# Running the attention products of two half-steps in one stretch, with all eight PSUM banks in one ring

## Chip, cores, metric

One core of one Trainium2 chip. The metric is the device time of one execution in microseconds (us), the median of several. The span in a profile (first to last instruction) is some 1.8 us shorter than the time. The traces are each of one execution.

## The reference, cut to what matters

A decayed linear attention over 4 batches, 8 heads, 768 tokens in blocks of 64, followed by a dense layer with a tanh GELU:

```python
for b in range(nb):                       # blocks of 64 tokens
    intra = einsum('bhic,bhjc->bhij', qb, kb) * Dmask
    intra = einsum('bhij,bhjd->bhid', intra, vb)
    inter = einsum('bhid,bhde->bhie', qb * lam_pow, kv_state)
    out[:, :, sl] = intra + inter
    kv_state = lam_block * kv_state + einsum('bhsd,bhse->bhde', kb_dec, vb)
x = out.transpose(0, 2, 1, 3).reshape(3072, 512)
return gelu(x @ w_in) @ w_out             # 512 -> 2048 -> 512
```

## The kernel before

The kernel works in 24 steps. A step is half of the heads of one superblock of 256 tokens. Each step has an attention stretch on TensorE: `scores` (S), the key-value products (K), the products of the masked scores of the step before with v (O), and the products with the carried state. S, K and O use 64x64 tiles of the array; the state products use all 128x128. PSUM is the memory that TensorE writes its products to; the kernel deals it out in eight banks, each with room for 128x512 fp32 numbers, and a bank can be written anew only when its last reader is done.

```python
ps_S = tile_pool(name="psS", bufs=1, space=PSUM)     # scores: two banks of their own
ps_M = tile_pool(name="psM", bufs=6, space=PSUM)     # everything else: six banks

def R(n, s):                  # one stretch: scores of n, products of n and s = n - 1
    scores(n)
    products(n, s)            # K of n, O and state products of s; then x_out on ScalarE
    causal(n)                 # VectorE masks the scores: one instruction of 128x1024
    ...
    update(n, 0)              # VectorE takes K into the state, GpSimd spreads it

for n in range(8, NSTEP + 1):
    ...
    prep(n + 2)               # q, k, v of step n+2 to fp16; q and k transposed by a DMA
    fill(2 if n <= 12 else 4) # so many pieces of the dense layer
    R(m, n - 1)
    fill(1)
    U(m)
    fill(2 if n in (8, 11) or n > 12 and n % 2 else 3)
```

Between the stretches `fill` issues pieces of the dense layer for the tokens that are done. A piece is about 0.87 us of TensorE. A group of two superblocks has 30 of them: 16 pieces of the first matmul (bank Hps, emptied by the GELU on ScalarE into gT) and then, twice, seven products named by their banks A, A, B, B, C, D, D. The second matmul is done in a Strassen-like form, with seven products in place of eight, so VectorE must first form sums of blocks of gT:

```python
G_SUMS = {5: ..., 2: ..., 1: ..., 7: ..., 6: ...}     # five sums; B needs 5 and 2, C needs 1, D 7 and 6
behind(9, 0, 4)       # behind piece 9: the five sums of blocks 0..3  (128x1024 each)
behind(13, 4, 6)      # behind piece 13: the five sums of blocks 4, 5 (128x512)
behind(n1, 6, 8)      # behind piece 16: the five sums of blocks 6, 7 (128x512)
```

## Time and profile before

| | before |
|---|---|
| median time | 205.1 us (204.85 to 205.55, 3 runs) |
| span of the profiled run | 202.8 us |
| busy: TensorE / VectorE / ScalarE / GpSimd | 96% / 72% / 53% / 33% |
| TensorE waits listed from 75 to 200 us | none |

A busy share of 96% alone is not proof, because matmuls overlap and their ends are modelled. In this study I use "pause" for the distance from one matmul's start to the next one's, less the time that the first needs to stream (216, 109 or 56 ns for 512, 256 or 128 columns). The waits that the profile lists are a little shorter, as they count from the modelled end.

This is VectorE's timeline over the two stretches of a group whose sums are being formed (start, length, instruction, count):

```profile
120.10 1.23 DVE L299 TENSOR_TENSOR PT<-Sps,mask 128x1024 f16<-128x1024 f32 x1 [4.72 <-PE Sps L290]
121.24 0.46 DVE L387 SCALAR_TENSOR_TENSOR t<-t,lamu,OK 128x64 f32<-128x64 f32 x2
122.25 4.01 DVE L469 TENSOR_TENSOR gs<-gT 128x1024 f16<-128x1024 f16 x5 [0.55 <-ACT gT L426]
126.18 0.68 DVE L240 TENSOR_TENSOR qk<-q,dq 128x512 f16<-128x512 f32 x1
126.79 1.75 DVE L469 TENSOR_TENSOR gs<-gT 128x512 f16<-128x512 f16 x5
128.46 1.21 DVE L299 TENSOR_TENSOR PT<-Sps,mask 128x1024 f16<-128x1024 f32 x1
...
130.40 2.72 DVE L469 TENSOR_TENSOR gs<-gT 128x512 f16<-128x512 f16 x4
```

### The profile page before, as it was taken

The numbers are of one execution on the slowest core, as the hardware profiler recorded it, in microseconds if no ns is written. First come the engines' busy times: TensorE is split into PE (matmuls) and PEld (weight loads), VectorE is DVE, ScalarE is ACT, GpSimd is POOL, SyncE is SP. The second block draws the span as 40 slices with busy tenths as digits, with TensorE's granted clock in tenths as the row PEclk, the third lists the DMA queues.
The fourth block names the chain that finished last, engine by engine and source line by source line (L and its number), as shares of the span: only waits on it lengthen the run. The fifth ranks groups of instructions, "written<-read, shape, count | busy, mean of one in ns | idle before, by whom it ended". The sixth has DMA issues, their size and how long they took to land.

```text
span 202.8 us, 5650 instructions
## 1 busy us (share of the span) xinstructions
PE 194.7 (96%) x2348; PEld 129.2 (64%) x2348; DVE 146.1 (72%) x281; ACT 108.1 (53%) x205; POOL 66.7 (33%) x80
## 2 busy tenths in 40 slices
PE   6888999999999999999999999999999999999993
PEld 1456544456887888654688654788554788545882
DVE  5896623889999989939997738996739673136653
ACT  2475778375793473487632477641576431666210
POOL 6593132457475354136135404315412100000000
PEclk9999999999999999999999999999999999999999
DMA  6999999999999999698669974775230003300014
GB/s 175 291 330 387 383 387 376 291 289 318 289 254 224 294 238 293 129 276 191 67 167 201 301 187 123 89 173 148 83 88 0 3 0 107 105 0 0 3 45 162
DMA packets 64201, 37.85 MB, mean 187 GB/s; under 512 B 17584, under 2 KB 59568, under 8 KB 64176
## 3 DMA queue, kind: packets, MB, share of 16 engines
q1 hardware_dynamic: 63344, 36.97, 71.3%
q10 hardware_dynamic: 832, 0.52, 0.9%
q8 instruction: 18, 0.29, 0.6%
q14 instruction: 7, 0.06, 0.1%
HBM read 27.26 MB, written 6.29 MB: 165 GB/s over the span
## 4 chain that ended last, share of the span: by engine, by line
PE 80%; DMA 10%; SPq 4%; ACT 2%; issue 1%; DVE 1%; ACTq 0%
PE Hps L422 34%; PE MD L493 8%; PE MB L493 8%; PE MA L493 7%; PE O2ps L437 6%; PE MC L493 4%; SPq L69 4%; DMA wi<-in_moe_w_in_dram 4%; DMA qkT<-qk 3%; PE Hps L539 3%; DMA out_dram<-o 3%; PE Sps L290 3%; PE OK L348 3%; PE OK L339 2%; ACT gT L426 1%
## 5 line engine op out<-in xcount | busy, mean ns | idle before, releaser
L422 PE MATMUL Hps<-xT,w_in 128*128 128x512 f16 (+1 forms) x416 | 79.1, 346 | 0.0
L426 ACT ACTIVATE gT<-Hps 128x512 f16<-128x512 f32 x88 | 52.2, 600 | 24.2 <-PE Hps L422 23.4
L422 PEld LDWEIGHTS <-w_in 128*128 128x128 f16 x416 | 40.1, 98 | 33.4
L394 POOL TENSOR_TENSOR u<-t,lumask 128x256 f16<-128x256 f32 x40 | 29.2, 734 | 81.9 <-DVE t L387 58.9
L469 DVE TENSOR_TENSOR gs<-gT 128x512 f16<-128x512 f16 (+1 forms) x74 | 43.3, 645 | 11.8 <-ACT gT L426 11.6
L493 PEld LDWEIGHTS <-gs 128*128 128x128 f16 x400 | 38.6, 98 | 4.7 <-DVE gs L469 0.3
L299 DVE TENSOR_TENSOR PT<-Sps,mask 128x1024 f16<-128x1024 f32 x24 | 29.2, 1216 | 13.1 <-PE Sps L290 13.1
L230 POOL TENSOR_TENSOR v<-v,dv 128x512 f16<-128x512 f32 x24 | 29.2, 1218 | 5.0 <-DMA v<-in_v_dram 3.3
L367 ACT ACTIVATE xT<-OK 128x256 f16<-128x256 f32 x47 | 18.2, 459 | 18.0 <-PE OK L348 14.6
L500 ACT ACTIVATE m<-MB 128x512 f32<-128x512 f32 x10 | 6.0, 597 | 27.7 <-PE MB L493 27.7
L493 PE MATMUL MA<-w_sum,gT 128*128 128x256 f16 x160 | 19.5, 273 | 0.1
L245 ACT ACTIVATE qk<-k 128x512 f16<-128x512 f32 x24 | 15.1, 629 | 8.1 <-DMA k<-in_k_dram 8.1
L493 PE MATMUL MD<-w_sum,gs 128*128 128x256 f16 x152 | 19.4, 273 | 0.0
L493 PE MATMUL MB<-w_out,gs 128*128 128x256 f16 x160 | 19.3, 273 | 0.0
L493 PEld LDWEIGHTS <-gT 128*128 128x128 f16 x160 | 15.5, 98 | 3.2 <-ACT gT L426 0.5
L240 DVE TENSOR_TENSOR qk<-q,dq 128x512 f16<-128x512 f32 x23 | 17.3, 754 | 0.0
L504 DVE TENSOR_TENSOR o<-MA,m 128x512 f32<-128x512 f32 x10 | 6.9, 686 | 12.0 <-ACT m L500 12.0
L387 DVE SCALAR_TENSOR_TENSOR t<-t,lamu,OK 128x64 f32<-128x64 f32 x64 | 14.7, 272 | 0.6
L437 PE MATMUL O2ps<-w_out,gT 128*128 128x512 f16 x64 | 14.6, 379 | 0.0
L128 DVE TENSOR_TENSOR w_sum<-w_out 128x1024 f16<-128x1024 f16 x10 | 8.9, 926 | 6.5 <-POOL w_out L118 3.5
L290 PEld LDWEIGHTS <-qkT 64*64 64x64 f16 x384 | 6.1, 106 | 8.8 <-issue 4.2
L290 PE MATMUL Sps<-qkT 64*64 64x128 f16 x384 | 10.0, 222 | 1.1 <-DVE qkT L266 0.5
(59 smaller groups left out, 158.1 us busy)
## 6 DMA issues: line engine op xcount, KB each, us to landing
q<-in_q_dram SPq DMA_DIRECT2D x24, 256.0 KB, 4.8
k<-in_k_dram SPq DMA_DIRECT2D x24, 256.0 KB, 4.8
v<-in_v_dram SPq DMA_DIRECT2D x23, 256.0 KB, 5.3
out_dram<-o SPq DMA_DIRECT2D x22, 256.0 KB, 3.4
wo<-in_moe_w_out_dram SPq DMA_DIRECT2D x4, 1024.0 KB, 9.5
wi<-in_moe_w_in_dram SPq DMA_DIRECT2D x4, 512.0 KB, 7.6
wi<-in_moe_w_in_dram SPq DMA_DIRECT2D x2, 1024.0 KB, 12.5
v<-in_v_dram ACTq DMA_DIRECT2D x1, 256.0 KB, 4.3
```

The source lines that it names most:

```text
L230: pin(nc.gpsimd.tensor_tensor(wide(tv[:]), ld32[s][2][:], decay(dv, s), ALU.mult))
L240: pin(q_eng.tensor_tensor(wide(tq), q32[:], decay(dq, s), ALU.mult))
L245: pin(nc.scalar.activation(out=wide(tk), in_=k32[:], func=AF.Copy))
L290: pin(nc.tensor.matmul(Sps[half64(c), hl, hp, jk, :], o[half64(hl), 1, jk, hp, half64(c)], o[half64(hl), 0, :, hp, half64(c)], start=True, ...
L299: pin(nc.vector.tensor_tensor(t[:].rearrange("p a b c d -> p (a b) (c d)"), Ss.pop(n)[:].rearrange("p a b c d -> p (a b) (c d)"), mask[:]. ...
L367: pin(nc.scalar.activation(out=d, in_=o, func=AF.Copy))
L394: pin(nc.gpsimd.tensor_tensor(u[:], state[half][:].unsqueeze(2).to_broadcast([P, 2, 2, D]), lumask[:, 2 * half : 2 * half + 2, :].unsqueez ...
L422: pin(nc.tensor.matmul(by_block(Hps[:, i, :]), w_in16[:, c, f * P : (f + 1) * P], x(c), start=(c == 0), stop=(c == NC - 1)))
L426: pin(nc.scalar.activation(out=dst, in_=Hps[:], func=AF.Gelu_apprx_tanh))
L437: pin(nc.tensor.matmul(O2[tau][0][:], gT[:, f % HF, f // HF, tau * P : (tau + 1) * P], w_out16[:, f, :], start=(n == 0), stop=(n == NF - 1)))
L469: pin(nc.vector.tensor_tensor(gsum[m][:, i, :], block(T0, F0, i), block(T1, F1, i), op))
L493: pin(nc.tensor.matmul(dst, lhsT, rhs, start=(i == 0), stop=(i == HF - 1), skip_group_check=True))
```

## The change

From step 10 on the two steps of a superblock go through one stretch, a burst: S of both, O of the two steps before, K of both, state products. This halves the number of changes between 64x64 and 128x128 tiles. A burst needs four banks for scores, two for O and two for K, so the two pools become one of eight banks, the score tile becomes two tiles, and the masking of a step becomes two instructions. The pieces between are dealt out anew.

```diff
-    ps_S = ctx.enter_context(tc.tile_pool(name="psS", bufs=1, space=PSUM))
-    ps_M = ctx.enter_context(tc.tile_pool(name="psM", bufs=6, space=PSUM))
+    ps_M = ctx.enter_context(tc.tile_pool(name="psM", bufs=8, space=PSUM))
 ...
+    def burst(ns, ss):
+        for n in ns:
+            scores(n)
+        O = [ps_M.tile([P, 2, 2, P], FP32, tag="M", name=f"O{c}") for c in range(2)]
+        ... # O of both ss
+        if ns:
+            K = [ps_M.tile([P, 2, P], FP32, tag="M", name=f"K{c}") for c in range(2)]
+        ... # K of both ns, then the state products of both ss
+        for n in ns:
+            causal(n)
+        for i, s in enumerate(ss):
+            x_out(s, [t[:, i].rearrange("p h t -> p (h t)") for t in O])
+        ...
+        for n in ns:
+            update(n, 0)
 ...
-    for n in range(8, NSTEP + 1):
-        ...
+    ... # steps 8 and 9 singly
+    for n in range(10, NSTEP + 1, 2):
+        ns = (n, n + 1) if n < NSTEP else ()
+        if n + 2 < NSTEP:
+            prep(n + 2)
+        fill(0 if n == 12 else 2)
+        burst(ns, (9,) if n == 10 else (n - 2, n - 1))
+        fill(2)
+        for m in ns:
+            U(m)
+        fill(2)
+        if n + 3 < NSTEP:
+            prep(n + 3)
+        fill(5 if n == 10 else 13 if n % 4 else 5)
```

More of the change, by code (lines that the diff above doesn't have):

```diff
@@ L285, in scores @@
         o = qkT[n]
-        Sps = ps_S.tile([P, 2, 2, 2, P], FP32, tag="S", name="Sps")
+        Sps = [ps_M.tile([P, 2, 2, P], FP32, tag="M", name=f"S{hl}") for hl in range(2)]
         for hp in range(2):
@@ L290, in scores @@
                     pin(nc.tensor.matmul(
-                        Sps[half64(c), hl, hp, jk, :], o[half64(hl), 1, jk, hp, half64(c)],
+                        Sps[hl][half64(c), hp, jk, :], o[half64(hl), 1, jk, hp, half64(c)],
                         o[half64(hl), 0, :, hp, half64(c)], start=True, stop=True,
@@ L298, in causal @@
         t = ptp.tile([P, 2, 2, 2, P], FP16, tag="PT", name=f"PT_{n}")
-        pin(nc.vector.tensor_tensor(
-            t[:].rearrange("p a b c d -> p (a b) (c d)"),
-            Ss.pop(n)[:].rearrange("p a b c d -> p (a b) (c d)"),
-            mask[:].unsqueeze(1).to_broadcast([P, 4, 2 * P]), ALU.mult))
+        for hl, Sps in enumerate(Ss.pop(n)):
+            pin(nc.vector.tensor_tensor(
+                t[:, hl].rearrange("p b c d -> p b (c d)"), Sps[:].rearrange("p b c d -> p b (c d)"),
+                mask[:].unsqueeze(1).to_broadcast([P, 2, 2 * P]), ALU.mult))
         PTs[n] = t
@@ L328, in products @@
                             start=start(c, hl), stop=(jk == 1), skip_group_check=True))
-            Kps[n] = OK
+            Kps[n] = [t[:, 256:384] for t in OK]
         if s is None:
@@ L353, in products, with start @@
         return OK, opened
+    def burst(ns, ss):
+        for n in ns:
+            scores(n)
+        O = [ps_M.tile([P, 2, 2, P], FP32, tag="M", name=f"O{c}") for c in range(2)]
+        seen = set()
+        def start(kind, c, hl):
+            new = (kind, c, hl) not in seen
+            seen.add((kind, c, hl))
+            return new
+        qTs = [qkT.pop(s) for s in ss]
+        for i, s in enumerate(ss):
+            PT, tv = PTs.pop(s), a16.pop(s)[2]
+            for hp in range(2):
+                for jk in range(2):
+                    for c, hl in TILES:
+                        pin(nc.tensor.matmul(
+                            O[c][half64(hl), i, hp, :], tv[half64(c), jk, 2 * hp + hl, :],
+                            PT[half64(c), hl, hp, jk, :], start=start("O", c, hl), stop=False,
+                            skip_group_check=True))
+        if ns:
+            K = [ps_M.tile([P, 2, P], FP32, tag="M", name=f"K{c}") for c in range(2)]
+        for i, n in enumerate(ns):
+            _, tk, tv = a16[n]
+            last = (n // 2) % NSB == NSB - 1
+            for jk in range(2):
+                for hp in range(2):
+                    for c, hl in TILES:
+                        if c == 1 and last:
+                            continue
+                        pin(nc.tensor.matmul(
+                            K[c][half64(hl), i, hp * D : hp * D + D],
+                            tk[half64(c), jk, 2 * hp + hl, :], tv[half64(c), jk, 2 * hp + hl, :],
+                            start=start("K", c, hl), stop=(jk == 1), skip_group_check=True))
+            Kps[n] = [t[:, i] for t in K]
+        for i, s in enumerate(ss):
+            for c in range(2):
+                if c == 0 and (s // 2) % NSB == 0:
+                    continue
+                u = us.pop((s, 0) if c else (s - 2, 1))
+                for hp in range(2):
+                    pin(nc.tensor.matmul(O[c][:, i, hp, :], u[:, hp].rearrange("p l d -> p (l d)"),
+                                         qTs[i][:, 0, :, hp, half64(c)], start=False, stop=True,
+                                         skip_group_check=True))
+        for n in ns:
+            causal(n)
+        for i, s in enumerate(ss):
+            x_out(s, [t[:, i].rearrange("p h t -> p (h t)") for t in O])
+        sbg = ss[-1] // 2
+        g, i = group_of[sbg]
+        if i == len(groups[g]) - 1:
+            queue_group(g)
+        for n in ns:
+            update(n, 0)
@@ L379, in update @@
         if "t" in parts:
-            OK = Kps[s] if c == 0 else Kps.pop(s)
-            K = OK[c][:, 256:384].rearrange("p (hp d) -> p hp d", hp=2)
+            K = (Kps[s] if c == 0 else Kps.pop(s))[c].rearrange("p (hp d) -> p hp d", hp=2)
             t = ucp.tile([P, 2, D], FP32, tag=f"t{half}", name=f"t_{s}_{c}")
@@ L711 @@
     fill(2)
-    for n in range(8, NSTEP + 1):
-        m = n if n < NSTEP else None
-        if m is not None:
-            stage_t(n)
+    stage_t(8)
+    prep(10)
+    fill(2)
+    R(8, 7)
+    fill(1)
+    U(8)
+    fill(2)
+    prep(11)
+    fill(2)
+    R(9, 8)
+    fill(1)
+    U(9)
+    fill(3)
+    for n in range(10, NSTEP + 1, 2):
+        ns = (n, n + 1) if n < NSTEP else ()
         if n + 2 < NSTEP:
             prep(n + 2)
-        fill(2 if n <= 12 else 4)
-        R(m, n - 1)
-        fill(1)
-        if m is not None:
-            U(m)
-        fill(2 if n in (8, 11) or n > 12 and n % 2 else 3)
+        fill(0 if n == 12 else 2)
+        burst(ns, (9,) if n == 10 else (n - 2, n - 1))
+        fill(2)
+        for m in ns:
+            U(m)
+        fill(2)
+        if n + 3 < NSTEP:
+            prep(n + 3)
+        fill(5 if n == 10 else 13 if n % 4 else 5)
     fill(len(filler))
```

## The prediction

> **What bounds the kernel now.** I read the page's busy shares and clock first, then the chain of waits, then TensorE's waits in the part that the change touches, and last the timeline around one attention stretch.
>
> ```profile
> PE 194.7 (96%) x2348; PEld 129.2 (64%) x2348; DVE 146.1 (72%) x281; ACT 108.1 (53%) x205; POOL 66.7 (33%) x80
> PEclk9999999999999999999999999999999999999999
> PE 80%; DMA 10%; SPq 4%; ACT 2%; issue 1%; DVE 1%; ACTq 0%
> ```
>
> TensorE is busy for 96% of the span, at full clock, and is 80% of the chain. A busy TensorE says little by itself, as its ends are modelled; the chain says more:
>
> ```profile
> 82.86 0.87 PE MD L493 x8
> 83.73 6.04 PE Hps L422 x28
> 89.78 0.35 PE Sps L290 x16
> 90.12 0.12 PE OK L325 x16
> 90.25 0.23 PE OK L339 x16
> 90.47 0.22 PE OK L348 x2
> 90.69 6.04 PE Hps L422 x28
> 96.73 0.35 PE Sps L290 x16
> ```
>
> From 77 us to the end every piece of the chain is a matmul, and each begins where the one before ended. Asked for TensorE's waits from 75 to 200 us, the profile lists none. So in the stretch where the change acts (step 10 starts at about 70 us) the time is the sum of TensorE's start-to-start times, and two things alone can change it: fewer nanoseconds between matmuls, or a wait that was not there. The 216 ns from one 128x512 matmul to the next (6.04 / 28) is streaming; it can't shrink. What is not streaming stands at the two ends of an attention stretch (64x64 tiles between 128x128 ones). Two narrow windows of TensorE's timeline show the starts:
>
> ```profile
> 89.40 0.38 PE L422 MATMUL Hps<-xT,w_in 128*128 128x512 f16 x1
> ```
>
> ```profile
> 90.25 0.22 PE L339 MATMUL OK<-PT,v 64*64 64x128 f16 x3
> 90.41 0.28 PE L348 MATMUL OK<-qkT,u 128*128 128x128 f16 x2
> 90.53 0.38 PE L422 MATMUL Hps<-xT,w_in 128*128 128x512 f16 x1
> ```
>
> With the first score matmul at 89.71, the entry takes 309 ns in place of 216: 93 ns lost. The second group of four scores comes 80 ns after the first, where the later ones are 56 ns apart: 24 more. The exit, from the last group of four (90.25) to the first 128x128 matmul (90.41), takes 158 ns where 56 would do: 102 lost. The matmul after that comes 66 ns on: 10 more. One stretch thus pays 93 + 24 + 102 + 10 = 229 ns for going into small tiles and back.
>
> **What the Trainium skill says.** "TensorEngine Tiling (Array Packing)", section Key Properties, says that changing the tiling mode drains the TensorE, while tiles within one mode run independently. The trace agrees: 93 and 102 ns at the two changes, and almost nothing between the scores, the K products and the O products, all in 64x64 tiles. "TensorE: Matmul & The Clock Gate", section Back-to-back issue gap, gives N / 2.4 + 2.5 ns; 216 and 56 ns for 512 and 128 columns agree. "PSUM — Partial Sum Buffer", section The four PSUM rules, has 8 banks and at most one per matmul output; no trace shows the count, but it is what the change spends whole. "SBUF — State Buffer", section Who interferes with whom, says that a VectorE instruction with two SBUF inputs contends with a GpSimd instruction that reads SBUF. The trace agrees: five sums of 128x512 took 1.75 us from 126.79 on with GpSimd quiet, and five took 3.06 us from 130.40 on with GpSimd at work.
>
> **The change part by part.**
> Removed: from step 8 on the kernel before has 17 stretches (16 steps and one closing). Afterwards there are 2 single ones (8, 9) and 8 bursts (10, 12, ... 24), so 7 fewer: 7 x 0.229 = 1.6 us of TensorE time, all of it on the path. The matmuls themselves stay, and so do the pieces of the dense layers between. The start up to step 7 keeps its order; only the score tile becomes two tiles in the common pool.
> Added on VectorE: the masking of one step becomes two instructions. Consecutive 128x512 fp32 ones start 0.60 us apart (133.98, 134.58, 135.18), while the one of 128x1024 takes 1.14 us (128.46 to 129.60). So 0.06 us per step, 1.4 us over 24 steps, on an engine at 72%: nothing on the path by itself.
> Moved: a burst with both halves takes 4 score banks, 2 for O and 2 for K, all eight. Before, the scores had two banks of their own, so six others always came from the ring. Now each bank of a burst must be given up by its last reader first, and the first pieces after it need its score banks, which VectorE has to mask. From the built kernel I took who wrote each bank last and who reads it last. A burst that starts at T has its scores done at T+0.47 (8 groups x 56 ns + 24), its O products at T+0.92, K then takes 0.26 (8 x 32 ns), and exit and state products 0.55.
>
> The tight places are bursts 12, 16 and 20, which stand directly behind the products A and B of a dense group. There one bank is the one of A, and its last reader is the second of VectorE's two output sums, which needs ScalarE's copies of B:
>
> ```profile
> 132.74 0.27 PE L493 MATMUL MB<-w_out,gs 128*128 128x256 f16 x1
> ```
>
> ```profile
> 133.05 0.60 ACT L500 ACTIVATE m<-MB 128x512 f32<-128x512 f32 x1 [2.38 <-PE MB L493]
> 133.54 0.38 ACT L501 ACTIVATE m<-MB 128x256 f32<-128x256 f32 x1
> ```
>
> ScalarE starts 0.31 us after the last B matmul starts, which is T+0.11. Its first copy ends at T+0.71, VectorE's first sum runs from T+0.75, the second from T+1.35 to T+2.02. Bank A is free at about T+2.05.
> Burst 20: K's second bank is A's. It is wanted at T+0.92 and free at T+2.05: 1.13 us of standstill. Afterwards the score banks are masked in time.
> Burst 12: the same 1.13 us; then VectorE also has the q of step 14 (0.6 us) ahead of its masking, so the first score bank comes free at T+3.25, while TensorE wants it at T+2.86: 0.4 more, 1.5 in all.
> Burst 16: K's second half isn't computed there, and bank A goes to the piece behind the burst, wanted at about T+1.83: 0.2, with 0.1 for bank B: 0.3.
> Bursts 10, 14, 18, 22 and 24 stand behind dense pieces whose banks ScalarE has long emptied: none.
> Sum of these: 1.5 + 0.3 + 1.1 = 2.9, rounded to 3.0.
>
> Also moved: a burst needs the transposed q and k of two steps at its start. From issue to landing the transposes take 3.1 / 4.5 / 6.9 us (least, median, most). Step 11's landed at 70.43 in the trace before, and the burst wants it at 70.2. Step 13's is issued only after four dense pieces behind burst 10, and burst 12 starts about 9.5 us after burst 10: a margin from +1 to -2 us. And behind bursts 14 and 18 VectorE has four maskings, updates and ten sums in a row, so the last sums may come after the product that needs them. I put these together at 0.5 us, since most have some slack and waits at burst 12 overlap.
>
> Total: 205.1 - 1.6 + 3.0 + 0.5 = 207.0; I record 206.8, a little nearer to no loss, because the piece counts with their special cases (0 at step 12, 5 at step 10, 13) look tuned on the chip.
>
> **Rivals.** First: the waits are absorbed and the saving stands alone, 205.1 - 1.6 = 203.5. For it: VectorE is idle for 28% of the span, and no TensorE wait shows now. Against it: the last A sum is bound by latency and not by load, and nothing before the burst can hurry it. Second: VectorE becomes the local bound, for from 80 to 110 us it is busy 25.94 of 30 us. Then the pieces behind every burst wait for masking or sums, 0.5 to 1 us more at five bursts, and the time is 209 to 211. Against it: from 140 to 170 us it is busy 19.50 of 30. Third: late transposes hold bursts 12 and 14 by 1 to 3 us each: 208 to 210. For it: the 6 us landings around 76 and 88 us; against: fewer loads are in flight then.
>
> **Range and chances.** The floor is 203.5, where all waits vanish; I can find no second saving, so faster by over 2% (under 201.0) gets 0.02. Over 2% slower (above 209.2) needs 5.7 us of waits, nearly twice the firm ones: 0.10. Within 2%: 0.88. The range is 203.7 to 209.2.
>
> **What would show it.** Ten stretches from step 8 on, each with about 93 and 102 ns at its ends; a TensorE wait of about 1.1 us at the K products of bursts 12 and 20, put down to VectorE's output sum; masking instructions of about 0.67 us; and the waits adding up to about 3 us. No wait above 0.3 us at a burst would make the first rival right; waits on transposes at steps 11, 13 or 15 the third; waits of dense pieces for masking or sums at most bursts the second. A cost per stretch other than 229 ns would show the saving mis-sized.

## The result and the profile after

| | before | after |
|---|---|---|
| median time | 204.97 us (204.24 to 205.55, 4 runs) | 212.12 us (211.53 to 213.02, 4 runs) |
| ratio | | 1.0354 (95%: 1.0303 to 1.0406) |
| span of the profiled run | 202.8 us | 211.2 us |
| stretches from step 8 on | 17 | 10 |

Ratios are the mean time of one kernel's runs over that of the other's runs of the same rounds, so they are not quite the ratios of the medians. Executions over 1.5% slower than the fastest of the same kernel are left out of the means. The change made the kernel 7.1 us slower.

The page of the kernel after, busy shares and the chain:

```profile
PE 196.7 (93%) x2348; PEld 130.8 (62%) x2348; DVE 152.0 (72%) x305; ACT 107.2 (51%) x205; POOL 66.8 (32%) x80
PE 63%; DVE 23%; DMA 6%; SPq 4%; issue 3%; ACT 1%; DVEq 0%
```

TensorE was 80% of the chain and is now 63%; VectorE was 1% and is 23%. So in parts of the run VectorE sets the pace. TensorE's waits over the whole run, longest in total first (us in total, times, longest):

```profile
PE MB L549 <- DVE gs L525: 3.9, 2, 2.2
PE S L289 <- DMA qkT<-qk: 2.1, 2, 1.6
PE idle L154 <- DVE ones L148: 1.5, 1, 1.5
PE K L387 <- DVE o L561: 0.8, 1, 0.8
```

The third belongs to the start and was there before, and of the second the kernel before had one wait of 0.4 us, at about 63 us. The others are new. The new pauses from step 10 on, from the starts in TensorE's timeline, in the first profile and in a second profile of the same kernel (run after_again); those under 0.2 us are left out:

| pause of TensorE | what it waits for | first profile | second |
|---|---|---|---|
| product B behind burst 14 | VectorE's block sum gs | 2.35 | 1.78 |
| product B behind burst 18 | the same | 1.86 | 1.98 |
| burst 10, scores of step 11 | DMA transpose of q and k | 0.69 | 0.64 |
| burst 12, scores of step 13 | the same | 1.74 | 2.59 |
| burst 14, scores of step 15 | the same | none | 0.68 |
| burst 20, K | bank of A, VectorE's output sum | 1.03 | 1.03 |
| behind burst 16 | the same | 0.22 | 0.22 |
| sum | | 7.9 | 8.9 |

Less the 7 x 0.229 = 1.6 us saved, the second profile should be 7.3 us over the span before; it is 210.5 - 202.8 = 7.7. In the first, 6.3 is expected and 8.4 found, and 1.7 of the rest is a fall of the clock: from 107.7 to 111.0 us the granted clock was half.

```profile
107.70:111.00 3.30, 3.30 (x18) 2.30 (x16) 1.89 (x3) 1.34 (x3) 0.00 (x0) 0.50 0.07 19
```

(Window; busy time and count of TensorE, its weight loads, VectorE, ScalarE, GpSimd; then the clock, here 0.50, and the DMA share.) Sixteen matmuls started 0.104 us too late there, 1.7 us in all. It isn't the cause of the slowdown: the second profile has a clock of 1.000, and its time, 212.26 us, is no shorter than the kernel's median.

The longest pause, in TensorE's timeline and then in VectorE's. Burst 14 starts at 93.03:

```profile
103.34 0.82 PE L549 MATMUL MB<-w_out,gs 128*128 128x256 f16 x6
106.35 1.26 PE L549 MATMUL MB<-w_out,gs 128*128 128x256 f16 x10 [2.19 <-DVE gs L525]
```

```profile
93.49 2.48 DVE L299 TENSOR_TENSOR PT<-S,mask 128x512 f16<-128x512 f32 x4 [3.87 <-PE S L289]
95.89 0.84 DVE L443 SCALAR_TENSOR_TENSOR t<-t,lamu,K 128x64 f32<-128x64 f32 x4
96.66 3.83 DVE L525 TENSOR_TENSOR gs<-gT 128x1024 f16<-128x1024 f16 x5
100.41 0.84 DVE L443 SCALAR_TENSOR_TENSOR t<-t,lamu,K 128x64 f32<-128x64 f32 x4
101.17 1.00 DVE L239 TENSOR_TENSOR qk<-q,dq 128x512 f16<-128x512 f32 x1
102.09 5.20 DVE L525 TENSOR_TENSOR gs<-gT 128x512 f16<-128x512 f16 x9
```

VectorE stands idle for 3.87 us before the burst, because the next instruction in its order, a masking, waits for the scores (experiment 5 shows that other work was ready), and then works without a break for over 13 us. Six matmuls of B are done by 103.34 + 6 x 0.109 = 103.99; the seventh needs the sum of block 6, which is the sixth of the row that starts at 102.09. The chain of waits gives those six 4.13 us, 0.69 each in the mean. In the kernel before, five such sums took 1.75 us (126.79), 0.35 each. GpSimd's timeline of the same stretch of the kernel after shows what runs beside them, and VectorE's, in narrow windows, shows that the mean hides two kinds of sums:

```profile
101.01 1.63 POOL L450 TENSOR_TENSOR u<-t,lumask 128x256 f16<-128x256 f32 x2 [2.88 <-DVE t L443]
...
102.61 1.22 POOL L229 TENSOR_TENSOR v<-v,dv 128x512 f16<-128x512 f32 x1
```

```profile
102.85 1.26 DVE L525 TENSOR_TENSOR gs<-gT 128x512 f16<-128x512 f16 x1
...
105.21 0.41 DVE L525 TENSOR_TENSOR gs<-gT 128x512 f16<-128x512 f16 x1
```

The first three of the six stand beside a GpSimd instruction each and end 0.28 to 0.29 us after it (102.92, 104.11 and 105.29, after 102.64, 103.82 and 105.00). From the start of each to the next one's are 0.76, 1.18 and 1.18 us; from 105.21 on, with GpSimd quiet, 0.34.

The other two pauses that matter, burst 12 (second half of the scores) and burst 20 (K):

```profile
79.91 0.42 PE L289 MATMUL S<-qkT 64*64 64x128 f16 x16
81.90 0.42 PE L289 MATMUL S<-qkT 64*64 64x128 f16 x16 [1.57 <-DMA qkT<-qk]
```

```profile
148.44 0.21 PE L387 MATMUL K<-v,qk 64*64 64x64 f16 x1
149.48 0.44 PE L387 MATMUL K<-v,qk 64*64 64x64 f16 x31 [0.83 <-DVE o L561]
```

### The profile page after: what moved, and what is told of

Read it like the earlier page. It is cut to its first block, busy times and chain, and to the rows that moved or that the text cites. A ratio compares the mean times of both kernels' runs of the same rounds, so it can differ in the third digit from the quotient of the medians.

```text
span 211.2 us, 5685 instructions
## 1 busy us (share of the span) xinstructions
PE 196.7 (93%) x2348; PEld 130.8 (62%) x2348; DVE 152.0 (72%) x305; ACT 107.2 (51%) x205; POOL 66.8 (32%) x80
## 4 chain that ended last, share of the span: by engine, by line
PE 63%; DVE 23%; DMA 6%; SPq 4%; issue 3%; ACT 1%; DVEq 0%
PE Hps L478 23%; DVE gs L525 9%; PE MD L549 8%; PE O2ps L493 7%; PE MB L549 6%; PE MA L549 5%; DVE PT L299 4%; PE MC L549 4%; SPq L68 4%; DMA wi<-in_moe_w_in_dram 3%; PE Hps L595 3%; DVE qk L239 3%; DVE t L443 2%; DMA qkT<-qk 2%; PE S L289 1%
## 5 line engine op out<-in xcount | busy, mean ns | idle before, releaser
L450 POOL TENSOR_TENSOR u<-t,lumask 128x256 f16<-128x256 f32 x40 | 28.4, 725 | 78.8 <-DVE t L443 46.3
L525 DVE TENSOR_TENSOR gs<-gT 128x512 f16<-128x512 f16 (+1 forms) x74 | 44.1, 658 | 9.2 <-ACT gT L482 9.2
L549 PEld LDWEIGHTS <-gs 128*128 128x128 f16 x400 | 39.4, 100 | 10.5 <-DVE gs L525 5.0
L299 DVE TENSOR_TENSOR PT<-S,mask 128x512 f16<-128x512 f32 x48 | 30.1, 680 | 12.3 <-PE S L289 12.3
L229 POOL TENSOR_TENSOR v<-v,dv 128x512 f16<-128x512 f32 x24 | 29.8, 1253 | 5.0 <-PE OK L324 1.7
L239 DVE TENSOR_TENSOR qk<-q,dq 128x512 f16<-128x512 f32 x23 | 20.5, 900 | 0.0
L424 ACT ACTIVATE xT<-O 128x256 f16<-128x256 f32 x30 | 10.7, 459 | 9.1 <-PE O L398 8.1
L289 PE MATMUL S<-qkT 64*64 64x128 f16 x384 | 9.4, 221 | 2.8 <-DMA qkT<-qk 2.1
L549 PE MATMUL MC<-w_sum,gs 128*128 128x256 f16 x80 | 11.0, 283 | 0.1
```

Source lines behind the costliest of these rows:

```text
L229: pin(nc.gpsimd.tensor_tensor(wide(tv[:]), ld32[s][2][:], decay(dv, s), ALU.mult))
L239: pin(q_eng.tensor_tensor(wide(tq), q32[:], decay(dq, s), ALU.mult))
L289: pin(nc.tensor.matmul(Sps[hl][half64(c), hp, jk, :], o[half64(hl), 1, jk, hp, half64(c)], o[half64(hl), 0, :, hp, half64(c)], start=True, ...
L299: pin(nc.vector.tensor_tensor(t[:, hl].rearrange("p b c d -> p b (c d)"), Sps[:].rearrange("p b c d -> p b (c d)"), mask[:].unsqueeze(1).t ...
L424: pin(nc.scalar.activation(out=d, in_=o, func=AF.Copy))
L450: pin(nc.gpsimd.tensor_tensor(u[:], state[half][:].unsqueeze(2).to_broadcast([P, 2, 2, D]), lumask[:, 2 * half : 2 * half + 2, :].unsqueez ...
```

## The experiments

Three theories after the result. **A**: the main loss is VectorE coming late with the block sums behind bursts 14 and 18, because the burst moves two maskings and two updates ahead of them, and perhaps because GpSimd then reads at the same time. **B**: the loss is in the banks: a burst wants all eight, or the common ring or the split masking costs by itself. **C**: transposes come late, because a burst wants two at once. All kernels below gave correct results unless it is said.

### Experiment 1: the urgent sums first

To the kernel after:

```diff
             behind(9, 0, 4)
-            behind(13, 4, 6)
-            behind(n1, 6, 8)
+            behind(13, 4, 6, (5, 2))
+            behind(n1, 6, 8, (5, 2))
+            behind(n1 + 1, 4, 8, (1, 7, 6))
```

> The changed kernel with the last sums of a dense group in another order: the two that the next two products need come first, the three others after them, in three instructions in place of six. Theory A (the main loss is VectorE reaching these sums too late, in its unbroken row of work behind bursts 14 and 18; 2.35 and 1.86 us in the trace): both waits of MB for gs fall to under 0.3 us and the time falls by about 4 us, to 208. Theory B (the loss is in the eight banks that a burst needs): nothing to win here, 212. Theory C (transposes that come late): 212 too.

Measured: 210.74 us (209.58 to 211.53), 1.0256 of before (1.0198 to 1.0315). B's pauses fell to 1.48 and 1.03, not to 0.3. The wanted sum is now the third of its row, not the sixth, but those three took 3.19 us (104.05 to 107.24): the first ended 0.28 us after GpSimd's spreading of the state, the other two 0.28 us after a scaling of v each. Theory A in part, and a hint that the neighbour and not only the order counts.

### Experiment 2: transposes earlier

To the kernel after, `prep(n + 3)` directly behind the burst, and `prep(11)` directly behind step 8:

```diff
         burst(ns, (9,) if n == 10 else (n - 2, n - 1))
+        if n + 3 < NSTEP:
+            prep(n + 3)
         fill(2)
         for m in ns:
             U(m)
         fill(2)
-        if n + 3 < NSTEP:
-            prep(n + 3)
```

> The changed kernel with the casts and the transpose of step n+3 placed directly behind burst n in place of four dense pieces later, and those of step 11 two pieces earlier. Theory C (bursts 10 and 12 wait for the transposed q and k of their second half, 0.69 and 1.74 us in the trace): both waits fall to under 0.4 us, and the time falls by up to 2.4 us, to about 210; where burst 12 no longer waits for the transpose, the wait for the bank of A that it hid may show, some 1 us, so 210 to 211. Theories A and B: no change, 212, or A a little worse because VectorE has the q ahead of the sums.

Measured: 213.56 us (212.62 to 214.34), 1.0396: no gain. TensorE's waits from 75 us on:

```profile
PE MB L549 <- DVE gs L525: 4.2, 2, 2.3
PE K L387 <- DVE o L561: 1.6, 2, 0.8
PE MC L549 <- DVE PT L299: 0.2, 1, 0.2
```

The transposes are gone from the list, but K now waits for the output sum twice: burst 12 pauses 0.97 us at K and 0.37 behind the burst, 1.34 in all. The prediction had 1.5 us for just this place. In the kernel after, that wait lay hidden behind the longer one for the transpose. The earlier `prep(11)` also made ScalarE wait for the load of k ahead of a GELU, and TensorE paused 1.85 us at 60 us; that is the edit's own fault. So theory C's waits are real, but the one at step 13 is worth far less than its length.

### Experiment 3: the ring without the bursts

The kernel before with only the pools, the score tiles and the masking of the change:

```diff
-        Sps = ps_S.tile([P, 2, 2, 2, P], FP32, tag="S", name="Sps")
+        Sps = [ps_M.tile([P, 2, 2, P], FP32, tag="M", name=f"S{hl}") for hl in range(2)]
 ... # ps_M with 8 banks, causal in two instructions, as in the change
```

> The kernel before, with only the pool part of the change: all eight banks in one ring, the scores in two tiles of it, the masking in two instructions; no bursts. If sharing the ring or the longer masking costs by itself (theory B in its wide form), the time rises by 1 us or more over 205. Theories A and C: within 0.5 us of 205.

Measured: 204.62 us (204.44 to 205.25), 0.9973 (0.9922 to 1.0024), the same as before, and no TensorE wait from 75 to 200 us. The shared ring and the split masking cost nothing. Theory B in its wide form falls.

### Experiment 4: experiments 1 and 2 together

> e1 and e2 together. If the losses are independent and A and C name them: 212 - 4.2 - 2.4 = about 205.5, with 1 to 1.3 us of bank waits (bursts 20 and 16) and the saving of 1.6 us in it. If they hide one another, 207 or more.

Measured: 210.24 us (209.39 to 210.84), 1.0233 (1.0182 to 1.0285). B's pauses are 1.48 and 1.03 as in experiment 1, K at burst 20 is 1.03, burst 12 still waits 0.97 for a transpose and then 0.37, and product B of the first group now waits 1.05 for its sums. The losses do not add; one gives way to the next.

### Experiment 5: half of the first sums before the burst

Experiment 1 with one more line changed:

```diff
-            behind(9, 0, 4)
+            behind(5, 0, 2)
+            behind(9, 2, 4)
```

> e1 with one more move: the first block of sums is cut in two, the half whose inputs are ready is done before the burst of steps 14 and 18, while VectorE stands idle there (3.9 us in the trace). Theory A (VectorE has too much to do between the burst and the product that needs the last sums): the waits of MB for gs, 2.35 and 1.86 us in the changed kernel and 1.48 and 1.03 in e1, fall below 0.3 us, and the time falls to about 208. Were the waits set by something else than VectorE's load there, they would stay at e1's 1 to 1.5 us and the time at 210.7.

Measured: 209.37 us (208.31 to 210.97), 1.022 (1.0153 to 1.0287). The waits from 86 us on:

```profile
PE K L387 <- DVE o L561: 0.8, 1, 0.8
PE MC L549 <- DVE PT L299: 0.2, 1, 0.2
```

The waits for sums are gone (one pause of 0.14 us is left at burst 14's product). Burst 12 still paused 1.1 us for its transpose. In this trace another 2.5 us were lost before 40 us, where nothing had been changed (ScalarE waited for loads of k for up to 3.1 us at a time), so it shows less than the whole gain; whether the other runs lost that too isn't on record. VectorE's idle time before the burst was the place for this work; with the load spread, the product does not wait.

### Experiment 6: bursts 16 and 20 at another place

The kernel after, with 15 and 15 pieces between bursts in place of 19 and 11:

```diff
-        fill(5 if n == 10 else 13 if n % 4 else 5)
+        fill(5 if n <= 12 else 9)
```

> The changed kernel with the dense pieces between bursts split 15 and 15 from step 14 on in place of 19 and 11, so that bursts 16 and 20 stand behind the last sum of a token block and not behind its product B. Theory B (K's bank waits for VectorE's sum of A): the waits at K of burst 20 (1.03 us) and behind burst 16 (0.22) vanish; MB's waits for gs stay near 2 us, as the place of bursts 14 and 18 is the same; so about 211. Theory A alone: 212.

Measured: 211.18 us, the median of the three fast runs (210.68 to 212.80; the fourth, 214.39, was slow), 1.0326 (1.027 to 1.0382). K's pause at burst 20 fell from 1.03 to 0.32 and the one behind burst 16 went away; B's pauses stayed at 2.48 and 2.04, and step 13's transpose at 2.25. The bank theory holds in its narrow form: the wait is set by where the burst stands behind product B, and it was worth 0.9 us at most. The median is 0.85 us below that of the kernel after (212.03, below), as forecast, but three runs that lie 2.1 us apart don't make this sure.

### Experiment 7: GpSimd without its reads

Wrong result (relative error 1.03):

```diff
-        pin(nc.gpsimd.tensor_tensor(wide(tv[:]), ld32[s][2][:], decay(dv, s), ALU.mult))
+        if s >= 10:
+            pin(nc.gpsimd.memset(tv[:], 0.0625))
+        else:
+            pin(nc.gpsimd.tensor_tensor(wide(tv[:]), ld32[s][2][:], decay(dv, s), ALU.mult))
```

> Wrong result on purpose: from step 10 on the scaling of v on GpSimd is replaced by a memset of the same tile, which reads no SBUF. If the sums come late because GpSimd's reading slows VectorE's two-input sums (ten of them took 0.65 us each in the changed kernel; 0.35 each where GpSimd was quiet before), they run at under 0.45 us, MB's waits fall from 2.35 and 1.86 to under 1 us each, and the time falls by about 3 us, to 209. If VectorE's row of work is too long whatever GpSimd does, the waits stay above 1.5 us and the time above 211.

Measured: 207.89 us (207.65 to 209.18), 1.016 (1.0121 to 1.0199), so 4.1 us less than the kernel after. The two rows of sums in the same part of VectorE's timeline:

```profile
96.55 3.83 DVE L528 TENSOR_TENSOR gs<-gT 128x1024 f16<-128x1024 f16 x5
...
102.00 3.85 DVE L528 TENSOR_TENSOR gs<-gT 128x512 f16<-128x512 f16 x10
```

The maskings, updates and the q between are within 0.02 us of the kernel after, and so are the first five sums, beside GpSimd's state spreading, which still reads. Only the last ten differ: 3.85 us, 0.385 each, where six had taken 4.13. The first of them still ended 0.28 us after the state spreading; two ran beside the memsets (102.49 to 103.47) and started the next after 0.34 us, as with GpSimd quiet. So it is the reading and not GpSimd's being at work. B's pauses fell from 2.35 and 1.86 to 0.73 and 0.20: without GpSimd's reading of v the product was late by under 1 us, with it by 2 us. What is left is not the row of VectorE in itself either. Beside the state spreading, two of the first five sums took 0.93 and 1.02 us to the next start in place of 0.60, the q 0.92 in place of 0.60 and one of the ten 0.75 in place of 0.34, 1.5 us together. That is more than the 0.73, so with no reading on GpSimd the product would not have waited: an estimate, which no run tests.

### Experiment 8: bursts from step 14 on

Steps 10 to 13 singly, as in the kernel before; sums as in experiment 5; bursts 16, 20 and 24 ahead of the second block's products:

```diff
-    for n in range(10, NSTEP + 1, 2):
+    for n in range(10, 14):
+        prep(n + 2)
+        fill(2 if n <= 12 else 4)
+        R(n, n - 1)
+        fill(1)
+        U(n)
+        fill(2 if n == 11 or n > 12 else 3)
+
+    for n in range(14, NSTEP + 1, 2):
 ...
-        fill(5 if n == 10 else 13 if n % 4 else 5)
+        fill(13 if n % 4 == 2 and n > 14 else 5)
```

> A version meant to keep the saving and lose the waits: bursts only from step 14 on (so no transpose is wanted early), bursts of steps 16, 20 and 24 placed ahead of the second token block's products, the sums ordered as in e5. 12 stretches from step 8 on in place of 17 save 5 x 0.229 = 1.1 us. If theories A, B and C name all the waits: 203.9, against 205 before. Any wait left is added to that: with 1 us of rest it equals the kernel before.

Measured: 206.58 us (206.38 to 208.53), 1.0105 (1.0053 to 1.0156). No transpose wait after step 9, but the group around burst 14 still waits for sums, 0.49, 0.30 and 0.78 us, and small pauses add up to some 1 us. Most of the loss is gone, not all of it.

### The kernel after once more

> The changed kernel once more, unaltered, for a second profile: in the first one TensorE's clock fell for 3.4 us behind the longest wait. If the waits are the kernel's own, the same four places wait again for about the same times (sums 2.4 and 1.9 us, transposes 0.7 and 1.7, the bank of A 1.0), whatever the clock does, and the time is 211.5 to 212.5.

Measured: 212.03 us (211.46 to 212.26), 1.034 (1.0307 to 1.0373). The same places wait; the figures are in the table above, and the transpose of step 15 comes to them. The clock was 1.000 throughout.

### Experiment 9: bursts from step 16 on

As experiment 8, with steps 10 to 15 singly, each five or six pieces apart.

> e8 with bursts only from step 16 on, where e8 still waited for sums of the group of step 14: 13 stretches in place of 17, a saving of 4 x 0.229 = 0.9 us. If no wait is left beyond those of the kernel before, 204.0 to 204.4 against 205; if the sums and banks still cost what they cost in e8, 205.5 to 206.

Measured: 205.85 us (204.91 to 206.6, 6 runs), 1.0044 (1.0011 to 1.0077): a little slower than the kernel before. New pauses of 0.60 (A waits for the output sum of D), 0.32 and 0.24 us take back the 0.9 us saved, and this trace also lost 1 us more than that of before at the start. The hoped-for gain did not come.

### Experiment 10: the opposite of the change

The kernel before, from step 10 on with a dense piece between scores and products:

```diff
         if n is not None:
             scores(n)
+        if n is not None and n >= 10:
+            fill(1)
         products(n, s)
 ...
-        fill(2 if n <= 12 else 4)
+        fill((2 if n <= 12 else 4) - (10 <= n < NSTEP))
```

> The kernel before with the opposite of the change: from step 10 on one dense piece is taken from ahead of the scores and put between the scores and the products, so that each of 14 steps goes into small tiles twice. If a stretch costs 0.2 to 0.23 us of TensorE time and nothing else matters, the time rises by 14 x 0.2 to 0.23 = 2.8 to 3.2 us, to about 208, and TensorE shows no new waits. If the cost per stretch is only an appearance of modelled ends, the time stays at 205.

Measured: 208.17 us (207.25 to 208.72), 1.0156 (1.0118 to 1.0195), 3.3 us more, and no TensorE wait from 75 us on. The pauses of TensorE from step 10 on add up to 6.78 us where they were 3.84 (a group of four 64x64 matmuls counted as one, pauses over 8 ns): 2.94 for 14 more stretches, 0.21 each. One of the split steps:

```profile
128.65 0.42 PE L290 MATMUL Sps<-qkT 64*64 64x128 f16 x16
129.00 1.04 PE L422 MATMUL Hps<-xT,w_in 128*128 128x512 f16 x4
129.96 0.32 PE L325 MATMUL OK<-v,qk 64*64 64x64 f16 x16
130.11 0.40 PE L339 MATMUL OK<-PT,v 64*64 64x128 f16 x16
```

Sixteen scores take 0.35 us to the next piece, and four matmuls of 512 columns take 0.96 where 4 x 0.216 = 0.86 would do: the two changes of tile size, a tenth of a microsecond each. The cost per stretch is real time.

### Experiment 11: a control

The kernel before with the sums of experiment 5.

> The kernel before with only the reordered sums of e5, without ring and bursts: a control for e8 and e9. It has no wait for sums, so nothing to win: within 0.5 us of 205, or a little worse.

Measured: 204.71 us (204.27 to 205.99, 6 runs), 0.9999 (0.9965 to 1.0033): the same. The order of the sums is worth nothing where nothing waits for them, so what it won in experiments 1 and 5 is repair of a loss that the bursts made.

No version beat the kernel before.

## Why the prediction was wrong

**The bound: right.** TensorE's start-to-start times set the time before. Experiment 11 and experiment 3 fit: other work on VectorE or in the banks, as long as nothing waits, changes nothing. ("To the end" is a little too wide: the chain is of matmuls up to 199.4 us, and the last 3.4 us are an output sum and its store.)

**The saving, 7 x 0.229 = 1.6 us: right.** The kernel after has 10 stretches from step 8 on, with 0.09 us lost at a clean entry and about 0.1 at every exit. Experiment 10 adds 14 stretches and pays 0.21 us of pauses each. By this count there was never more than this to win.

**The split masking off the path: right.** Four took 2.40 us to the next instruction, 0.60 each as worked out, and experiment 3 shows it costing nothing. In the row behind a burst it adds 4 x 0.60 - 2 x 1.14 = 0.12 us.

**The bank waits, 3.0 us: right in mechanism, too large in sum.** Burst 20: 1.13 predicted, 1.03 measured. Burst 16: 0.3 predicted, 0.22 measured. Burst 12: 1.5 predicted, nothing seen, because a longer wait for the transpose stood ahead of it and the bank was free by then; experiment 2 took that wait away and 1.34 us of the predicted one appeared. So 1.25 in place of 3.0.

**The step that failed is "I put these together at 0.5 us", for late transposes and late sums.** They measured 2.4 + 4.2 = 6.6 us in the first profile and 3.9 + 3.8 = 7.7 in the second. The text had named both and waved both through with "most have some slack". Nothing was added up for the sums, though the trace before had every duration: 4 maskings x 0.60, 8 updates x 0.20, five sums 4.01, the q 0.61, and six sums at 0.61 to 0.35 give 2.4 + 1.6 + 4.0 + 0.6 + 2.1 to 3.7 = 10.7 to 12.3 us. From the first masking at T + 0.46 that is T + 11.2 to 12.8, against a product that wants its sum at T + 10.96 (103.99 - 93.03, in the trace after): 0.2 to 1.8 us at each of two bursts, an estimate. The measured row was longer again, T + 13.3, because the six sums took 4.1 us and the q 0.9. The contention with GpSimd, which the prediction cites, was not carried into this sum. In the trace after, the instructions that stood beside a reading GpSimd instruction in this row (two of the first five sums, the q, three of the six) cost 3.2 us more by their starts than the same ones elsewhere; without that, an estimate, the sum would have been there 0.9 us before it was wanted. Experiment 7 shows the larger part of it: with the v scaling made harmless, the time falls by 4.1 us and the pauses by 3.3.

For the transposes the margin at burst 12 was given as "+1 to -2 us" and then counted as nearly nothing; the waits there were 1.74 and 2.59 us.

**The rivals.** The second (VectorE as a local bound) and the third (late transposes) were both right in kind and came together. Each had been given its own total, 209 to 211 and 208 to 210. Their places were partly wrong: VectorE held product B behind two bursts for about 2 us each, not the pieces behind five bursts for 0.5 to 1 us, and transposes held bursts 10 and 12, and 14 in one trace of two. The weight against the second was that VectorE is busy for only 19.50 of 30 us later on. That was the wrong measure: at burst 14 VectorE was idle for 3.87 us just before the row of over 13 us began. A mean over 30 us cannot see this. And "no wait shows now" told nothing of how much room there was: 0.3 and 0.9 us at product B.

**The tuned look of the piece counts** had drawn the estimate a little towards the old time. It was no evidence.

**What stays open.** Why no placing with bursts came out ahead isn't settled: experiments 8 and 9 took the large waits away, and then pauses of 0.2 to 0.8 us at other places used up the 0.9 to 1.1 us saved. A better placing may exist, for at most 1.6 us. How far the half clock in four traces follows from the pauses isn't settled either.

## What to carry to other kernels

When a change makes one engine's work lumpier, add up the next engine's row of work, instruction by instruction, from the moment it may start to the moment when somebody needs its last result; a busy share, even of a 30 us window, does not show it. Use the durations that hold beside the neighbours that will run then, not the quiet ones. And weigh the prize first: here at most 1.6 us was to be won by using up all eight banks and every margin that the old order had held, and a wait that is removed may only uncover the one behind it.

## What the Trainium skill lacked or had wrong

- "TensorEngine Tiling (Array Packing)", Key Properties, says that a change of mode drains the TensorE, but not what it costs. Here: 93 + 24 ns on the way into 64x64 tiles and 102 + 10 ns on the way out, 0.21 us of pauses for each stretch added in experiment 10.
- "SBUF — State Buffer", Who interferes with whom, has the rule that was at work here and no size for such sums. Sums of two fp16 inputs of 128x512 took 0.34 us to the next start with GpSimd quiet or in a memset, and up to 1.19 beside its reading instructions of 0.6 to 1.2 us. That section calls the port that the two share an exclusive lock, and the traces agree: the sums beside a scaling of v ended 0.28 to 0.29 us after it. Only the mean over a row, 0.69 us, looks like a slower rate.
- "DMA: Bandwidth & Descriptors", DMA Transpose (X-bar), gives no latency. Here a transpose of q and k of one step took 3.1 to 6.9 us from issue to landing (median 4.5 in the kernel before).
- "TensorE: Matmul & The Clock Gate", HAM oscillation — how this bites in real kernels, gives "no PE-idle gaps >~3.4µs" as the abstract rule. In four traces here (the first of the kernel after, and experiments 1, 2 and 6) the granted clock was half for some 3 us, from 0.2 to 1.3 us after the end of a pause of only 2.2 to 2.5 us (no cause shown); after pauses of 2.59 and 2.48 us in the second trace of the kernel after and in experiment 6 it stayed whole.
